# Left queries of dilated heads on two key blocks, slot sums with the dispatch weights stationary, and 512-wide early w2 products

## The chip, the cores and the metric

The kernel runs on one core of a Trainium2 chip. The metric is the device time of one execution in microseconds (us). The kernel before takes 181.05 us, the median of three runs (180.69, 181.05 and 181.62). Inputs and the result lie in HBM as 32-bit floats; the kernel works on 16-bit floats, and the transfers convert.

## The reference

A sliding-window attention is followed by a soft mixture of experts. Eight batches, eight heads, 576 positions, head dimension 64. Heads 0 to 3 ("plain") see the last 32 positions; heads 4 to 7 ("dilated") see every fourth of the last 128.

```python
scores = scale * np.matmul(q, k.transpose(0, 1, 3, 2))
mask_plain = (rel >= 0) & (rel < window)                               # window 32
mask_dil = (rel >= 0) & (rel < window * dilation) & (rel % dilation == 0)   # dilation 4
attn = softmax of the masked scores
x = (attn @ v), rows (batch, position), 512 columns: head by head

logits = x @ phi                       # 4608 x 32: 8 experts with 4 slots each
d = softmax of logits over the rows    # dispatch
slot_input = d.T @ x                   # 32 x 512
slot_out[e] = np.maximum(slot_input[e] @ w1[e], 0.0) @ w2[e]   # w1: 512 x 1024, w2: 1024 x 512
c = softmax of logits over the slots   # combine
return c @ slot_out                    # 4608 x 512
```

In bytes: q, k and v are 9.4 MB each, w1 and w2 together 33.6 MB, the result 9.4 MB.

## The kernel before

**Loads.** Every load of q, k, v and the weights is issued by POOL, and converts to 16 bits on the way; a load or store waits on POOL's queue for the data it needs, for the buffer it fills, and for the transfer issued eight before it, since there are eight completion semaphores. The order is fixed by the program: raw q, k and v of batches 0 and 1, then those of batch b+2 as the transposes of batch b free the raw buffers, one w1 matrix after each batch from the fourth, and after batch 7 the rest of the weights. w2 of experts 5 to 7 come in column halves: first the left halves of all three, then the right halves.

**Attention.** DVE transposes the raw tiles in 32x32 blocks (`turn`, L222), so that the head dimension lies on the partitions. PE turns v back into rows of keys (`v_rows`, L237, through the rotating PSUM buffers `ring`), and ACT copies them beside a column of ones into `vX`. Scores come in nine pieces per batch: P0 to P4 are 128 keys of the plain heads and the up to 160 queries that see them; D0 to D3 are every fourth key of the first 512, from residue r, with the 144 queries of that residue; L is the "left" piece, the last 64 keys of the dilated heads with the last 64 queries, reordered by residue. Three groups of pieces (`GROUPS`) share one PSUM tile each (L263), one exponential on ACT (L272) and one product with a 0/1 mask on DVE (L283).

`emit_av` (L292 to L321) multiplies the probabilities, as stationary operand, with the rows of `vX`. The ones give the sum of the row, which `emit_recip` (L325) inverts and `norm_mult` (L328 to L346) applies, on ACT for some pieces and on DVE for others; the results are the rows of x in `xp` (plain) and `xd` (dilated). The left queries of the dilated heads see keys of their residue in the D pieces (columns 128 to 143) and in L. That gives 32 small products per batch: for each head and residue one with 64 keys of L and one with 128 keys of D, 16 columns wide.

**Experts' front.** PE transposes x (`xT_plain`, `xT_dil`), ACT copies it, PE forms the logits, and ACT their exponentials `ET` (slots on partitions). For the slot sums `back_erow` (L409) turns `ET` back into rows, with the left queries a second time by residue; `back_er` multiplies with a mask, and DVE transposes the dilated order (`back_erd`, L434). `back_u` (L437) makes 25 products per batch: a 128x128 block of x stationary, 32 columns of weights moving, and five with a block of ones for the sum of the weights. The sums, with x's columns on the partitions, are added up in `UT`.

**Order.** `ORDER` (L48) is a list written by hand: each entry is a step and the iteration by which it lags; all engines' instructions are issued in that order.

**The end.** After the last batch the slot inputs are normalised into `siTm` (L593 to L606), then come the products with w1 (L616), ReLU, a transpose, and the products with w2 (`emit_so`, L641): experts 0 to 3 and 4 as soon as those are loaded, in two column halves, then 5, 6 and 7 for the left half. `gather_so` and `spread_so` sum four partial results. `emit_batch` (L689) forms the result rows of one batch, scales them on ACT and DVE in turn (L681, L685), and POOL issues the store (L692). The right halves of experts 5 to 7 are worked in between these batches; left halves of six batches are stored first, then their right halves, then batches 6 and 7 whole, and last the left queries' rows (L721).

Of the kernel before, what the change touches and what calls it, by code (L numbers as in the profile page):

```python
# [17 lines left out]
S = 576  # L18
# [14 lines left out]
NV = 10  # L33
# [3 lines left out]
DW = 144  # L37
LEFT = SUB - 128
# [6 lines left out]
    (("P", 3), ("P", 4), ("L", 0), ("D", 0)),  # L45
# [12 lines left out]
WIDTH = {"P": PW, "L": DIL * LEFT, "D": DW}  # L58


def piece_w(kind, i):
    return S - 512 if (kind, i) == ("P", 4) else WIDTH[kind]

# [15 lines left out]
def make_consts():  # L79

    a = np.arange(128)[:, None]
    rel = np.arange(PW)[None, :] - a
    band = (rel >= 0) & (rel < WINDOW)
    one = np.ones((1, N_SLOTS), bool)
    r, i = np.divmod(np.arange(DIL * LEFT)[None, :], LEFT)
    parts = [band, (a < 64) & (a % DIL == r) & (a // DIL <= i)]
    parts.append(((a % 32) < LEFT) & one)
    parts.append((a < 64) & one)
# [7 lines left out]
def kernel(  # L96
# [18 lines left out]
    band, lmask = cst[:, 0:PW], cst[:, PW : PW + DIL * LEFT]  # L115
    o_em = PW + DIL * LEFT
    o = o_em + 2 * N_SLOTS
# [4 lines left out]
    emask = consts.tile([128, 6, N_SLOTS], FP16, name="emask")  # L122
    phi_raw = consts.tile([128, 4, N_SLOTS], FP16, name="phi_raw")
    phi4 = consts.tile([128, 4, 4, N_SLOTS], FP16, name="phi4")
    ones = consts.tile([128, 128], FP16, name="ones")
    ET = consts.tile([128, 192 * B], FP16, name="ET")
    UT = consts.tile([128, 5, N_SLOTS], FP32, name="UT")
    rcol = consts.tile([128, N_SLOTS], FP32, name="rcol")
# [27 lines left out]
    x_pool = tc.alloc_tile_pool(name="xp", bufs=2)  # L156
# [12 lines left out]
    def build_masks():  # L169
# [8 lines left out]
        for kind, i in GROUPS[1]:  # L178
            w = piece_w(kind, i)
            copies(o, lmask if kind == "L" else band, w, 1)  # L180
            o += w
        nc.scalar.copy(
            out=emask[:, 4:6, :], in_=cst[:, o_em : o_em + 2 * N_SLOTS].rearrange("p (t s) -> p t s", t=2)
        )
# [39 lines left out]
    V_PARTS = ((0, 1, 2), (3, 4), (5, 6, 7), (8, 9))  # L224

    def v_rows(b, part):
        tiles = V_PARTS[part]
        rg = ring.tile([128, len(tiles), 4, 2, 32], FP16, name=f"rv_{b}_{part}", tag="ring")
        for n_t, t in enumerate(tiles):
            for c in range(2):  # L230
# [4 lines left out]
                else:  # L235
                    rows = vT[:, 1, 512:SK, c]
# [10 lines left out]
    def emit_scores(b, g):  # L247
        kb, qb = kT[b % 2], qT[b % 2]
        sps = psum_s.tile([128, 4, 512], FP32, name=f"s_{b}_{g}", tag="s")
        for kind, i in GROUPS[g]:  # L250
            c0, w = PIECE[(kind, i)][1], piece_w(kind, i)
            for tt in range(2):
                for h in range(4):
# [5 lines left out]
                    elif kind == "D":  # L259
                        kk, qq = kt[:, i:512:DIL], qt[:, i:S:DIL]  # L260
                    else:
                        kk, qq = kt[:, 512:SK], qt[:, 512:S].rearrange("p (i r) -> p r i", r=DIL)
# [11 lines left out]
    def emit_mask(b, g):  # L274
# [4 lines left out]
        else:  # L279
            m = masks[:, 0 : GW[0]].rearrange("p (n w) -> p n w", n=3)[:, :, 0:DW]  # L280
            m = m[:, None, :, :].broadcast_to([128, 4, 3, DW])
# [8 lines left out]
    xp_t, xd_t = {}, {}  # L290

    def emit_av(b, kind, i):  # L292
        o = psum_o.tile([128, 4, D + 1], FP32, name=f"o_{b}_{kind}{i}", tag="o")
        jobs, vb = [], vX[b % 2]
        for h in range(4):
            if kind == "L":
                for r in range(DIL):
                    p = probs(b, "L", 0, h, LEFT * r, 32)[0:64]
                    jobs.append((slice(32 * r, 32 * r + 32), p, vb[0:64, 9, h, 0 : D + 1], h))
            else:  # L300
                lhs = probs(b, kind, i, h, 0, 128)
                jobs.append((slice(0, 128), lhs, vb[:, i + (NP if kind == "D" else 0), h, 0 : D + 1], h))
        for h in range(4):
# [3 lines left out]
            elif kind == "L":  # L307
                for r in range(DIL):
                    lhs = probs(b, "D", r, h, 128, LEFT)
                    rows = slice(32 * r, 32 * r + LEFT)  # L310
                    jobs.append((rows, lhs, vb[:, NP + r, h, 0 : D + 1], h))
        for n, (rows, lhs, rhs, h) in enumerate(jobs):
# [4 lines left out]
                start=(n == 0 or (kind == "L" and n < DIL)),  # L317
# [5 lines left out]
    def emit_recip(b, kind, i, o):  # L323
        rc = s_pool.tile([128, 4], FP32, name=f"rc_{b}_{kind}{i}", tag=f"rc{kind}{i}")
        nc.vector.reciprocal(out=rc, in_=o[:, :, D])  # L325
        return rc

    def norm_mult(b, kind, i, o, rc, engine):  # L328
        pool, name = (xp_t, "xp") if kind == "P" else (xd_t, "xd")
        if b not in pool:  # L330
            pool[b] = x_pool.tile([128, 5, 4 * D], FP16, name=f"{name}_{b}", tag=name)
        dst = pool[b][:, 4 if kind == "L" else i, :]
        dst = dst.rearrange("p (c h d) -> p h c d", c=2, h=4)
        src = o[:, :, 0:D].rearrange("p h (c d) -> p h c d", c=2)
        if engine is nc.scalar:
# [8 lines left out]
            in1=rc[:, :, None, None].broadcast_to([128, 4, 2, D // 2]),  # L344
# [6 lines left out]
    def x_half(b, kind, t, c):  # L351
        return (xp_t if kind == "P" else xd_t)[b][:, t, 128 * c : 128 * c + 128]

    def xT_plain(b, c):
        rg = ring.tile([128, 640], FP16, name=f"rp_{b}_{c}", tag="ring")
        for t in range(NP):
            nc.tensor.transpose(rg[:, 128 * t : 128 * t + 128], x_half(b, "P", t, c), ident)  # L357
        return rg

    def xT_dil(b, c):  # L360
        rg = ring.tile([128, DIL, 160], FP16, name=f"rd_{b}_{c}", tag="ring")
        for r in range(DIL):
            nc.tensor.transpose(rg[:, r, 0:128], x_half(b, "D", r, c), ident)
        nc.tensor.transpose(rg[:, :, 128:160], x_half(b, "D", DIL, c), ident)
        return rg

    def xT_copy(b, kind, c, rg):
# [3 lines left out]
        if kind == "P":  # L371
            copy(out=xT_t[b][:, c, :], in_=rg[:, 0:S])  # L372
# [3 lines left out]
            in_=rg[:, :, 0:SUB].rearrange("p r i -> p i r"),  # L376
# [33 lines left out]
    def back_erow(b):  # L410
        m, l = et_cols(b)
        ep = ring.tile([128, 6, N_SLOTS], FP16, name=f"ep_{b}", tag="ring")
        left = ET[0:32, l : l + 128]
# [3 lines left out]
        nc.tensor.transpose(ep[:, 5, :], left, ident[0:32, 0:32])  # L417
        for r in range(DIL):
            nc.tensor.transpose(
                ep[32 * r : 32 * r + 32, 4, :],  # L420
                left.rearrange("p (i r) -> p r i", r=DIL)[:, r, :],
                ident[0:32, 0:32],
            )
        return ep

    def back_er(b, ep):
        er = s_pool.tile([128, 6, N_SLOTS], FP16, name=f"er_{b}", tag="er")
# [332 lines left out]
```

## Time and profile before

| what | before |
|---|---|
| median of three runs | 181.05 us |
| the profiled execution: its time, its span | 180.9 us, 178.9 us |
| busy: PE, DVE, ACT, POOL | 128.0, 125.7, 122.2, 56.2 us |
| PE: matmuls and as many weight loads | 2,316 |
| left rows of dilated heads (`o_L`, L313): matmuls | 256, 5.2 us |
| slot sums (`u`, L451): matmuls | 200 |
| early and late w2 products (`so`, L646): matmuls | 128 |
| HBM read, written | 62.07 MB, 9.44 MB |

The span runs from the first to the last instruction on the core. Busy times are unions: two instructions of one engine that overlap count once. A matmul's duration holds its way through the array, so matmuls of 200 ns can follow each other every 40 ns. The page has a row for the DMA engines: the core has 16 of them, and each transfer is spread over all; bytes are counted as they are in the 16-bit form for loads.

### The profile page before, as it was taken

How to read it: one execution, taken by the hardware profiler on the slowest of the kernel's cores; microseconds unless marked ns; L12 is line 12 of the kernel's file. 1: busy time of each engine (PE TensorE's matmuls, PEld its weight loads, DVE VectorE, ACT ScalarE, POOL GpSimd, SP SyncE). 2: the span in 40 equal slices, each digit the busy share in tenths (PEclk: the TensorE clock that was granted, in tenths of full speed). 3: DMA queues.
4: the chain of work that ended last, by engine and by line, in shares of the span. 5: the costliest groups of instructions: out<-in, count | busy, mean ns of one | idle time of the engine just before them, and what ended most of it. 6: DMA issues, size and time to landing. Idle time of an engine off the chain costs nothing.

```text
span 178.9 us, 5405 instructions
## 1 busy us (share of the span) xinstructions
PE 128.0 (72%) x2316; PEld 84.7 (47%) x2316; DVE 125.7 (70%) x274; ACT 122.2 (68%) x267; POOL 56.2 (31%) x94
## 2 busy tenths in 40 slices
PE   0026838989999999989989999988695346688100
PEld 0014525676667767657767757856434112221000
DVE  6483999999999999999999995472402016789200
ACT  6007757999999999999999999966002016698100
POOL 7544244224224223243420041111112414376400
PEclk9999999999999879999999999687669955555555
DMA  5999999999999999999999999999999999999994
GB/s 91 203 213 208 214 212 210 214 212 216 214 212 213 215 212 215 214 212 216 210 214 215 212 218 220 215 216 220 211 212 191 197 196 219 390 319 397 406 413 135
DMA packets 21448, 40.88 MB, mean 229 GB/s; under 512 B 1713, under 2 KB 14129, under 8 KB 20785
## 3 DMA queue, kind: packets, MB, share of 16 engines
q0 software_dynamic: 21280, 40.41, 114.2%
q8 instruction: 18, 0.29, 0.6%
q1 hardware_dynamic: 144, 0.14, 0.3%
q14 instruction: 6, 0.04, 0.1%
HBM read 62.07 MB, written 9.44 MB: 400 GB/s over the span
## 4 chain that ended last, share of the span: by engine, by line
DMA 52%; DVE 16%; PE 11%; ACT 9%; issue 3%; POOL 2%; POOLq 0%; DVEq 0%
DMA w<-in_moe_w_dram 36%; DMA rawV<-in_v_dram 10%; DMA rawK<-in_k_dram 6%; DVE vT L222 5%; DVE qk L222 4%; DVE p L283 3%; PE f L672 3%; ACT p L272 3%; ACT om L681 2%; PE s L263 2%; PE o_P L313 2%; PE rv L237 2%; ACT xp L337 1%; PE rp L357 1%; ACT vX L243 1%
## 5 line engine op out<-in xcount | busy, mean ns | idle before, releaser
L272 ACT ACTIVATE p<-s 128x1728 f16<-128x1728 f32 (+1 forms) x24 | 42.0, 1749 | 10.7 <-PE s L263 10.6
L263 PE MATMUL s<-qk 32*128 32x144 f16 (+2 forms) x640 | 29.2, 325 | 16.1 <-DVE qk L222 12.3
L313 PEld LDWEIGHTS <-p 128*128 128x128 f16 (+3 forms) x672 | 23.9, 101 | 14.0 <-issue 3.6
L263 PEld LDWEIGHTS <-qk 32*128 32x128 f16 x640 | 17.0, 118 | 20.4 <-DVE qk L222 12.3
L337 ACT ACTIVATE xp<-o_P,rc_P 128x64 f16<-128x64 f32 x96 | 23.8, 384 | 2.4 <-DVE rc_P L325 2.3
L283 DVE TENSOR_TENSOR p<-p,masks 128x1728 f16<-128x1728 f16 (+1 forms) x24 | 25.4, 1082 | 0.0
L243 ACT COPY vX<-rv 128x512 f16<-128x512 f16 (+1 forms) x32 | 23.5, 786 | 1.7 <-PE rv L237 1.6
L313 PE MATMUL o_P<-vX,p 128*128 128x65 f16 (+1 forms) x288 | 20.7, 210 | 1.3 <-DVE xp L341 0.3
L222 DVE STREAM_TRANSPOSE qk<-rawQ 128x576 uint32<-128x576 uint32 x16 | 18.9, 1243 | 2.7 <-DMA rawQ<-in_q_dram 2.7
L222 DVE STREAM_TRANSPOSE qk<-rawK 128x576 uint32<-128x576 uint32 x16 | 19.7, 1241 | 0.5 <-DMA rawK<-in_k_dram 0.5
L222 DVE STREAM_TRANSPOSE vT<-rawV 128x576 uint32<-128x576 uint32 x16 | 19.6, 1238 | 0.4 <-DMA rawV<-in_v_dram 0.4
L237 PE MATMUL rv<-cst,vT 128*128 128x128 f16 x160 | 17.3, 248 | 3.0 <-DVE vT L222 1.7
L211 POOL DMA_DIRECT2D w<-in_moe_w_dram x12 | 8.9, 745 | 29.1 <-DMA w<-in_moe_w_dram 24.8
L685 DVE TENSOR_SCALAR om<-f,rrow 128x256 f16<-128x256 f32 (+1 forms) x28 | 13.5, 518 | 3.9 <-PE f L672 3.1
L237 PEld LDWEIGHTS <-vT 128*128 128x128 f16 x160 | 12.0, 127 | 8.6 <-issue 4.3
L191 POOL DMA_DIRECT2D rawQ<-in_q_dram x16 | 8.9, 557 | 21.5 <-DVE rc_P L325 16.3
L681 ACT ACTIVATE om<-f,rrow 128x256 f16<-128x256 f32 (+1 forms) x28 | 12.8, 503 | 3.3 <-PE f L672 2.6
L672 PE MATMUL f<-so_sb,ET 32*128 32x256 f16 (+1 forms) x60 | 12.1, 420 | 3.7 <-ACT om L681 2.4
L692 POOL DMA_DIRECT2D out_dram<-om x14 | 10.4, 747 | 12.1 <-DVE om L685 9.4
L191 POOL DMA_DIRECT2D rawK<-in_k_dram x16 | 8.7, 548 | 17.1 <-DVE rc_P L325 14.6
L191 POOL DMA_DIRECT2D rawV<-in_v_dram x16 | 8.7, 547 | 10.8 <-DVE rc_P L325 8.0
L372 ACT COPY xT<-rp 128x576 f16<-128x576 f16 x16 | 10.5, 776 | 1.2 <-PE rp L357 1.2
(84 smaller groups left out, 197.4 us busy)
## 6 DMA issues: line engine op xcount, KB each, us to landing
w<-in_moe_w_dram POOLq DMA_DIRECT2D x13, 1024.0 KB, 21.7
out_dram<-om POOLq DMA_DIRECT2D x12, 512.0 KB, 6.2
rawQ<-in_q_dram POOLq DMA_DIRECT2D x16, 288.0 KB, 10.7
rawK<-in_k_dram POOLq DMA_DIRECT2D x16, 288.0 KB, 10.4
rawV<-in_v_dram POOLq DMA_DIRECT2D x16, 288.0 KB, 10.2
w<-in_moe_w_dram POOLq DMA_DIRECT2D x12, 256.0 KB, 16.4
out_dram<-om POOLq DMA_DIRECT2D x2, 1024.0 KB, 8.6
out_dram<-om_l POOLq DMA_DIRECT2D x2, 512.0 KB, 9.1
```

Source lines behind the costliest of these rows:

```text
L191: nc.gpsimd.dma_start(out=t[g::2, :], in_=src[4 * g : 4 * g + 4].rearrange("h (p j) d -> (h p) (j d)", j=PJ),)
L222: nc.vector.transpose(out=out_, in_=in_)
L237: nc.tensor.transpose(rg[:, n_t, :, c, :], rows, ident)
L243: copy(out=vX[b % 2][:, t0 : t0 + n, :, 0:D], in_=rg.rearrange("p n h c d -> p n h (c d)"))
L263: nc.tensor.matmul(sps[:, h, c0 : c0 + w], kk, qq, start=(tt == 0), stop=(tt == 1))
L272: return nc.scalar.activation(out=pt, in_=sps[:, :, 0:n], func=AF.Exp, scale=SCALE)
L283: return nc.vector.tensor_tensor(out=pt, in0=pt, in1=m, op=ALU.mult)
L313: nc.tensor.matmul(o[rows, h, :], lhs, rhs, start=(n == 0 or (kind == "L" and n < DIL)), stop=(n == len(jobs) - 1), skip_group_check=True,)
L337: nc.scalar.activation(out=dst[:, h], in_=src[:, h], func=AF.Copy, scale=rc[:, h : h + 1])
L672: nc.tensor.matmul(fp[:, 0 : c1 - c0], ET[32 * j : 32 * j + 32, m : m + 128], so_sb[32 * j : 32 * j + 32, c0:c1], start=True, stop=True,)
L681: nc.scalar.activation(out=dst, in_=fp[:, 0 : c1 - c0], func=AF.Copy, scale=rrow[:, blk : blk + 1])
L685: nc.vector.tensor_scalar(out=dst, in0=fp[:, 0 : c1 - c0], scalar1=rrow[:, blk : blk + 1], scalar2=None, op0=ALU.mult)
```

## The change

Four things are done, and the constants follow them.

- The left queries of the dilated heads are scored in natural order against two blocks of 128 keys, from 448 and from 384, as two pieces of group 1 (`LKEY`); the D pieces have 128 queries each. The second block counts only its first 64 keys. `v_rows` makes two row tiles for them where there was one, and `emit_av` needs 8 products per batch, into 64 rows.
- Rows that hold only 64 positions are computed as 64, and the transposes of x follow. x lies in fixed tiles with a column of ones behind its 256 columns.
- In `back_u` the dispatch weights are the stationary operand, and x with its ones is the moving one, 257 columns wide: 10 products per batch into 64 rows, plain and dilated below each other. The sums lie with slots on partitions, so at the end they are normalised by a column, transposed by PE, and copied into `siTm` by DVE (plain) and ACT (dilated).
- The w2 products of experts 0 to 4 are 512 columns wide, into one PSUM tile; experts 5 to 7 stay in halves.

```diff
-    (("P", 3), ("P", 4), ("L", 0), ("D", 0)),
+    (("P", 3), ("P", 4), ("L", 0), ("L", 1), ("D", 0)),
...
-WIDTH = {"P": PW, "L": DIL * LEFT, "D": DW}
+WIDTH = {"P": PW, "L": LEFT, "D": 128}
+LKEY = (448, 384)
...
-    V_PARTS = ((0, 1, 2), (3, 4), (5, 6, 7), (8, 9))
+    V_PARTS = ((0, 1, 2), (3, 4), (5, 6, 7), (8, 9, 10))
...
-                    rows = vT[:, 1, 512:SK, c]
+                    k0 = LKEY[t - NP - DIL]
+                    rows = vT[:, 1, k0 : k0 + 128, c]
...
-                    kk, qq = kt[:, 512:SK], qt[:, 512:S].rearrange("p (i r) -> p r i", r=DIL)
+                    kk, qq = kt[:, LKEY[i] : LKEY[i] + 128], qt[:, 512:S]
...
             if kind == "L":
-                for r in range(DIL):
-                    p = probs(b, "L", 0, h, LEFT * r, 32)[0:64]
-                    jobs.append((slice(32 * r, 32 * r + 32), p, vb[0:64, 9, h, 0 : D + 1], h))
+                for n in range(2):
+                    k = 128 if n == 0 else 64
+                    lhs = probs(b, "L", n, h, 0, LEFT)[0:k]
+                    jobs.append((slice(0, LEFT), lhs, vb[0:k, NP + DIL + n, h, 0 : D + 1], h))
...
-            elif kind == "L":
-                for r in range(DIL):
-                    lhs = probs(b, "D", r, h, 128, LEFT)
-                    rows = slice(32 * r, 32 * r + LEFT)
-                    jobs.append((rows, lhs, vb[:, NP + r, h, 0 : D + 1], h))
...
-        nc.tensor.transpose(ep[:, 5, :], left, ident[0:32, 0:32])
-        for r in range(DIL):
-            nc.tensor.transpose(
-                ep[32 * r : 32 * r + 32, 4, :],
-                left.rearrange("p (i r) -> p r i", r=DIL)[:, r, :],
-                ident[0:32, 0:32],
-            )
+        nc.tensor.transpose(ep[:, 4, :], ET[0:32, l : l + 128], ident[0:32, 0:32])
...
-        nc.vector.tensor_tensor(out=er, in0=ep, in1=emask, op=ALU.mult)
+        nc.vector.tensor_copy(out=er, in_=ep)
...
-        up = ring.tile([128, 5, N_SLOTS], FP32, name=f"u_{b}", tag="ring")
+        up = ring.tile([64, 4 * D + 1], FP32, name=f"u_{b}", tag="ring")
...
+            for k, x in enumerate((xp_t[b % 2], xd_t[b % 2])):
+                e = erd[:, t, :] if k == 1 and t < 4 else er[0:n, t, :]
+                nc.tensor.matmul(
+                    up[32 * k : 32 * k + 32, :],
+                    e,
+                    x[0:n, t, 0 : 4 * D + 1],
+                    start=(t == 0),
+                    stop=(t == NP - 1),
+                )
...
+    nc.vector.reciprocal(out=rcol, in_=U[:, 4 * D : 4 * D + 1])
+    nc.vector.tensor_scalar(out=si, in0=U[:, 0 : 4 * D], scalar1=rcol, scalar2=None, op0=ALU.mult)
+    for k, copy in enumerate((nc.vector.tensor_copy, nc.scalar.copy)):
+        siT = ring.tile([128, 2, N_SLOTS], FP16, name=f"siT{k}", tag="ring")
+        rows = slice(32 * k, 32 * k + 32)
+        for c in range(2):
+            nc.tensor.transpose(siT[:, c, :], si[rows, 128 * c : 128 * c + 128], ident[rows, rows])
...
+        copy(out=diag, in_=siT.rearrange("p c (e s) -> p c e s", e=E_EXP))
...
-    so = [psum_so.tile([128, DH], FP32, name=f"so{s}", tag=f"so{s}") for s in range(2)]
+    so = psum_so.tile([128, DMODEL], FP32, name="so", tag="so")
...
-    for s in range(2):
-        emit_so(s, (0, 1, 2, 3))
-    for s in range(2):
-        emit_so(s, (4,))
+    emit_so(None, (0, 1, 2, 3))
+    emit_so(None, (4,))
     for e in (5, 6, 7):
         emit_so(0, (e,))
```

More of the change, by code (lines that the diff above doesn't have):

```diff
@@ L32 @@
 PJ = S // PB
-NV = 10
+NV = 11
 SUB = S // DIL
@@ L83, in make_consts @@
     band = (rel >= 0) & (rel < WINDOW)
[L84 to L88, printed above, removed]
+    parts = [band]
+    for first in LKEY:
+        rel = 512 + np.arange(LEFT)[None, :] - first - a
+        seen = LKEY[0] if first < LKEY[0] else S
+        parts.append((rel >= 0) & (rel < WINDOW * DIL) & (rel % DIL == 0) & (first + a < seen))
     parts.append(a == np.arange(128)[None, :])
@@ L114 @@
     cst = consts.tile([128, consts_np.shape[1]], FP16, name="cst")
[L115 to L117 removed]
+    o = PW + 2 * LEFT
+    band, lmask = cst[:, 0:PW], [cst[:, PW + LEFT * i : PW + LEFT * i + LEFT] for i in range(2)]
     ident = cst[:, o : o + 128]
@@ L316, in emit_av @@
                 rhs,
-                start=(n == 0 or (kind == "L" and n < DIL)),
+                start=(n == 0),
                 stop=(n == len(jobs) - 1),
@@ L371, in xT_copy @@
         if kind == "P":
-            copy(out=xT_t[b][:, c, :], in_=rg[:, 0:S])
+            copy(out=xT_t[b][:, c, :], in_=rg)
             return
```

126 lines of the change are left out of this document (55 added, 71 removed).

## Prediction

> **What bounds the kernel now.** I read the summary page first: the slices of the span, the DMA queues and the issue table.
>
> ```profile
> span 178.9 us, 5405 instructions
> PEclk9999999999999879999999999687669955555555
> DMA  5999999999999999999999999999999999999994
> GB/s 91 203 213 208 214 212 210 214 212 216 214 212 213 215 212 215 214 212 216 210 214 215 212 218 220 215 216 220 211 212 191 197 196 219 390 319 397 406 413 135
> q0 software_dynamic: 21280, 40.41, 114.2%
> q8 instruction: 18, 0.29, 0.6%
> ...
> w<-in_moe_w_dram POOLq DMA_DIRECT2D x13, 1024.0 KB, 21.7
> ...
> rawQ<-in_q_dram POOLq DMA_DIRECT2D x16, 288.0 KB, 10.7
> rawK<-in_k_dram POOLq DMA_DIRECT2D x16, 288.0 KB, 10.4
> rawV<-in_v_dram POOLq DMA_DIRECT2D x16, 288.0 KB, 10.2
> ```
>
> The DMA row is full in all slices but the first and the last. A 288 KB load lands 10 us after its issue, yet loads land 1.4 us apart: some 8 us of work always stand queued ahead of it. So the transfers are the bound, and an engine matters only if it lets that queue run dry. The chain of waits says the same of the last third: weights back to back until 153.58, then a short run through the engines.
>
> ```profile
> 88.68 28.72 DMA w<-in_moe_w_dram
> 117.40 0.28 issue
> 117.68 25.39 DMA w<-in_moe_w_dram
> 143.08 0.28 issue
> 143.36 10.22 DMA w<-in_moe_w_dram
> 153.58 0.04 issue
> 153.62 0.43 PE so L646 x4
> ```
>
> Next, the completion marks in the trace: each transfer leaves 16, one for each DMA engine. This is the lag of the engines behind the first to finish, in order (us), for three loads, and then the marks of three outputs by their absolute time:
>
> ```
> load issued  22.23: 0.00 0.03 0.05 0.12 0.13 0.17 0.22 0.29 0.38 0.39 0.45 0.47 0.48 0.53 0.60 1.29
> load issued 117.68: 0.00 0.13 0.26 0.28 0.31 0.51 1.09 1.17 2.13 2.26 2.41 2.62 2.68 2.69 2.81 3.66
> load issued 143.36: 0.00 0.11 0.27 0.29 0.31 0.52 1.11 1.19 2.15 2.27 2.42 2.63 2.69 2.70 2.82 3.47
> output 5, issued 154.14: 1st 157.63, 14th 159.58, 15th 160.26, last 160.63
> output 6, issued 157.61: 1st 160.62, 14th 160.98, 15th 161.66, last 161.88
> last output, issued 167.93: 1st 176.13, 14th 176.46, 15th 177.10, last 177.39
> ```
>
> The engines carry equal bytes but drift apart. What differs are the 18 instruction packets of queue 8, 16,384 bytes and about 0.94 us each on one engine. They start at 22.1, 35.0, 42.5 and so on to 128.6, 140.7 and 154.0, each after about 256 further PE instructions (4,649 in the program). After the first, one engine is 0.7 us late; after seven, seven engines are; after sixteen, eight are late by 2.1 to 2.8. The 17th, at 140.7, makes one of these 3.66 late, and the 18th, at 154.0, holds up a second. So refills go round eight engines, and the two that were hit three times land last to the end. They never wait for an issue, so their load sets the time.
>
> **The change, part by part.** By the instruction listing of the two programs, the transfers, their order and what each waits for are the same. The constants stay 548 columns wide. So the byte floor does not move. What moves:
>
> PE instructions. Per batch, pairs of weight load and matmul: left rows 32 to 8 (-24), left scores +8, V transposes +2, transposes of the dispatch weights 6 to 2 (-4), slot sums 25 to 10 (-15), in all -33. Over eight batches -264; early w2 products 80 to 40 (-40); four new transposes (+4): -300 pairs, -600 instructions, 4,649 to 4,049. At 256 per refill that is 15.8, so 15 or 16 refills instead of 18. The 17th and 18th, the two that give an engine a third hit, do not happen. Without the 17th the worst lag at the end of the loads is 2.82 instead of 3.47: -0.65 us. Without both, the end is set by what is now the third slowest engine: at output 5 it is 160.63 - 159.58 = 1.05 ahead, at the last output 177.39 - 176.46 = 0.93 (from output 6 on it is partly held by the issues, so this is a lower bound). I take -1.0 us. A 16th refill, if there is one, is the second hit of the eighth engine, which it had before, and costs nothing.
>
> The Trainium skill, on the page "Runtime: NRT & Kernel Launch", section Instruction fetch mechanics, says that instructions are refilled in 16 KiB blocks of 256 and that crossing a block boundary is "mostly hidden"; by that the refills are worth nothing and the time would stay at 181.05. The block size agrees with the packets here; the hiding does not agree with the marks, since these transfers share engines that have no idle time.
>
> Work per batch on the engines, all of it beside the transfers. PE: the left rows took 0.67 us by the chain, about 0.2 after; slot sums 0.8 us before, and 10 products of 257 columns at 0.1 us (four 256-wide products took 0.40 at half clock) 0.5 to 1.0 after; two V transposes +0.2, four fewer small ones -0.2; eight more 64-wide scores +0.25 (3.9 us for 128), 32 narrower ones about -0.25. PE gains 0.3 to 0.8. ACT: the widths of the three exponentials sum to the same (1,344); one V copy grows from 512 to 768, 892 - 680 ns = +0.21 us. DVE: the sum over 257 columns takes at most the 0.40 of a 256-wide product instead of 0.30, `er` about 0.04 less, masks sum to the same. So a batch is 0.2 us longer at most if ACT sets its pace, 1.7 us over eight. Cover: the 8 us of queue; loads per batch take 6 x 1.4 + 4.9 = 13.3 us against some 12.9 between issues now. The added memsets (about 0.09 us each) replace two of 0.22 and 0.17 before the first load lands.
>
> The front of the expert part, once. The reciprocal and the product on 128 rows (0.35 + 0.29 us) become a reciprocal (0.17), a product of 256 columns (0.40), two transposes (0.25 each), a copy (0.27), and for the second half a wait of PE for the buffer that `rs` holds until DVE has read it (0.37), two more transposes, an ACT copy (0.27). That is about 2.0 us plus hops: +1.4 to +2.0. Behind PE's wait stand all w1 products. The 512-wide products move the same columns as before; at full clock nothing, at the 0.50 granted around them at most +1.5 us. With 0 to 1.7 us from the batches, the early products end later by d = 1.4 to 5.2 us. PE's own timeline shows the cover:
>
> ```profile
> 137.03 2.79 PE L646 MATMUL so<-w,hTm 128*32 128x256 f16 x88 [0.52 <-DVE hTm L628]
> 140.94 0.29 PE L646 MATMUL so<-w,hTm 128*32 128x256 f16 x4 [1.11 <-DMA w<-in_moe_w_dram]
> 143.12 0.38 PE L646 MATMUL so<-w,hTm 128*32 128x256 f16 x4 [1.88 <-DMA w<-in_moe_w_dram]
> 144.26 0.40 PE L646 MATMUL so<-w,hTm 128*32 128x256 f16 x4 [0.76 <-DMA w<-in_moe_w_dram]
> 145.64 0.41 PE L646 MATMUL so<-w,hTm 128*32 128x256 f16 x4 [0.98 <-DMA w<-in_moe_w_dram]
> ```
>
> That is 4.7 us of waiting for weights; 4.05 when they land 0.65 earlier. Then the first output, issued at 149.31, may be later too. Output 6 shows that an idle engine lands 3.0 us after an issue, 1.3 of it the transfer; the slowest engine is free at about 152.9, so an issue by 151.2 costs nothing: 1.9 more. Cover is lost at d = 6.0. I cost the front at nothing.
>
> After the last weight lands, the steps to output 6 are unchanged, so it should be issued 0.65 us earlier, at about 156.96; the slowest engine then ends output 5 at 159.6 and needs it by 157.9.
>
> Sum: 180.9 us of the profiled execution (span 178.9, 2.0 around it) less 1.0 is 179.9. The median of the runs, 181.05, is 0.15 above that execution: 180.05.
>
> **Rivals.**
> Refills hidden or replaced: lighter engines lose slack that I don't see, or other queues fill the place. For it: the instruction queue has 0.6% of the DMA time; against it: the jumps of 0.7 to 1.0 us in the marks. 181.05.
> One hit only: a different start of the round, or a refill late in the output phase, leaves one engine with a third hit; only 0.65 is won: 180.4. For it: the 18th refill came when PE had started 4,564 instructions, so the counting is loose by some tens; against it: 4,049 is 303 short of a 17th refill.
> Compute gets faster and the kernel follows: against it, no load waits for anything but the queue; no time of its own.
> Slower: the front of the expert part outlasts its cover. PE stands behind the new transposes and the first output comes late. It decides from d = 6.0 us, and each further us is a us on all output; at d = 8.5, 180.05 + 2.5 = 182.55. For it: PE's clock fell to 0.50 there, and ACT and DVE are busy without a gap from 36 to 108 us; against it: my worst d is 5.2, and PE is relieved in every batch.
>
> **How the numbers follow.** The three runs of before span 0.5%, and 0.5% (0.9 us) is about what a measurement of this kernel can tell from no change; the forecast stands just beyond that, at -0.55%. Chances: forecast 0.49 (its own range 179.6 to 180.3), one hit only 0.18, hidden refills 0.22, slower 0.11. So faster by over 0.5% 0.49, within 0.5% 0.40, slower 0.11. The range reaches from 179.5 (the gain at 1.05 and half of the spread of the runs) to 181.5 (hidden refills and the same spread); it leaves out most of the slower case.
>
> **What would show it.** Queue 8 with 15 or 16 packets; worst lag of the last load near 2.8; last weight near 152.9, last output near 176.4; all loads still 1.4 and 4.9 us apart. If PE no longer waits for `w` before the last early products, the slower case has come. Refills down with the last landing unmoved would make the central step wrong; so would a load that lands late after its issue into an empty queue.

## The result, and the profile after

The changed kernel takes 184.89 us, the median of six runs (181.99 to 187.23); the kernel before, run beside it, 180.9 us (180.68 to 181.62). The ratio is 1.0106, with a 95% interval of 1.006 to 1.0152. A second set gave 184.14 us (four runs, 182.91 to 186.09) against 181.2, a ratio of 1.0141 (1.0099 to 1.0184). The ratios leave out the runs that count as slow (four of the change's six here, one of its four in the second set), which is why they lie below the ratios of the medians, 1.022 and 1.016. So the change makes the kernel slower by 1.0 to 1.4% by the ratios and by 1.6 to 2.2% by the medians, where 0.55% faster was forecast. The runs spread over 5 us, where those of before spread over 1.

The profiled execution is the fastest of the six, 181.99 us. These are the lines of its summary page that answer those shown of before, with PE's busy time and its busy slices, and the shares of the chain of waits by engine:

```profile
span 180.1 us, 4810 instructions
...
PE 136.0 (75%) x2016; PEld 87.9 (49%) x2016; DVE 127.1 (71%) x277; ACT 125.2 (69%) x268; POOL 56.2 (31%) x94
...
PE   0015938999998998999899999998977687688000
...
PEclk9999999955999999987987955899955898555555
DMA  5999999999999999999999999999999999999994
GB/s 101 189 207 209 211 213 212 211 214 216 213 213 215 213 211 213 214 213 213 211 217 214 213 216 224 218 215 209 220 207 191 196 196 144 402 354 393 406 412 111
...
q0 software_dynamic: 21280, 40.41, 113.6%
q8 instruction: 16, 0.26, 0.5%
...
PE 39%; ACT 28%; DVE 13%; DMA 9%; issue 3%; POOL 1%; POOLq 0%; ACTq 0%; DVEq 0%
...
w<-in_moe_w_dram POOLq DMA_DIRECT2D x13, 1024.0 KB, 20.8
...
rawQ<-in_q_dram POOLq DMA_DIRECT2D x16, 288.0 KB, 10.1
rawK<-in_k_dram POOLq DMA_DIRECT2D x16, 288.0 KB, 8.6
rawV<-in_v_dram POOLq DMA_DIRECT2D x16, 288.0 KB, 9.0
```

Three things are to be seen. Queue 8 has 16 packets, as forecast. But PE is busy for 136.0 us with 2,016 products, where it was 128.0 with 2,316: a product has become dearer. And the clock row, which stood at 9 through most of the attention before (8 and 7 in two slices, lower at its end), now has more gaps, at the ninth and tenth slice and from the eighteenth on, while PE's own row stands at 8 or 9 there. The GB/s row has its answer in slice 34: 144, where it was 219.

The chain of waits ran through the transfers for 52% of the span before; now that is 9%, and PE has 39%. At the end of the attention and in the front of the expert part it reads:

```profile
132.82 0.34 ACT ET L408
133.21 0.29 PE ep L413
133.67 0.25 DVE er L421
133.97 1.39 PE u L437 x10
135.38 0.43 DVE U L451
...
137.15 5.61 PE hps L605 x53
...
145.43 3.03 PE so L636 x64
148.48 0.30 DVE so_part L651
...
150.00 0.47 ACT om L672
```

These are compute steps one behind the other, with no wait for a weight between them. PE's timeline shows the same place (start, duration, and in brackets the idle time before and what ended it):

```profile
137.08 5.64 PE L605 MATMUL hps<-w,siTm 128*32 128x512 f16 x64
...
145.43 3.00 PE L636 MATMUL so<-w,hTm 128*32 128x512 f16 x64 [0.52 <-DVE hTm L617]
```

The early w2 products start at 145.43 instead of 137.03, so d, the delay that the prediction put at 1.4 to 5.2 us, is 8.4. They run as one block of 64, with the left halves of experts 5 to 7 in it: no wait for `w` is left of the 4.7 us that stood here. That is the sign that the prediction named for the slower rival.

What became of the transfers is in their completion marks (us):

```
                                          before    after
last weight load, last mark               153.58   152.97
worst lag of one engine in that load        3.47     2.81
output 1, issued                          149.31   151.54
output 1, last mark                       154.97   154.95
output 5, last mark                       160.63   160.15
output 6, issued                          157.61   158.61
output 6, last mark                       161.88   161.88
output 8, last mark                       164.54   164.56
output 9, last mark                       165.92   167.12
last output, last mark                    177.39   178.64
instruction packets of queue 8           18, last at 154.0    16, last at 164.6
```

The loads end 0.6 us earlier, as the refill step said. Then output 1 is issued 2.2 us later: all engines have run dry by then, its marks lie within 0.37 us instead of 2.7, and the gain is gone. Output 6, issued 1.0 us later, meets a second hole, which before had stood on the faster engines alone: now the slowest one is free at 160.15, too. After eight outputs the two kernels are level to 0.02 us. The remaining 1.2 us come at one step, between outputs 8 and 9: there the 16th instruction packet, at 164.6, occupies one engine for 1.04 us. At output 8 the 16 marks lie within 0.28 us; from output 9 to the end one mark stays 0.9 to 1.2 us behind the other fifteen.

### The profile page after: what moved, and what is told of

The parts are those of the page before. It is cut to its first block, busy times and chain, and to the rows that moved or that the text cites. A ratio compares the mean times of both kernels' runs of the same rounds, so it can differ in the third digit from the quotient of the medians.

```text
span 180.1 us, 4810 instructions
## 1 busy us (share of the span) xinstructions
PE 136.0 (75%) x2016; PEld 87.9 (49%) x2016; DVE 127.1 (71%) x277; ACT 125.2 (69%) x268; POOL 56.2 (31%) x94
## 4 chain that ended last, share of the span: by engine, by line
PE 39%; ACT 28%; DVE 13%; DMA 9%; issue 3%; POOL 1%; POOLq 0%; ACTq 0%; DVEq 0%
ACT p L271 10%; PE s L262 7%; DMA phi_raw<-in_moe_phi_dram 5%; PE o_L L307 5%; ACT xp L331 5%; PE f L663 4%; DVE qk L220 4%; ACT xT L374 4%; PE o_P L307 4%; DMA rawK<-in_k_dram 4%; PE u L437 3%; PE hps L605 3%; ACT vX L242 3%; ACT om L672 3%; PE rv L236 3%
## 5 line engine op out<-in xcount | busy, mean ns | idle before, releaser
L271 ACT ACTIVATE p<-s 128x1920 f16<-128x1920 f32 (+1 forms) x24 | 41.4, 1726 | 12.5 <-PE s L262 12.3
L262 PE MATMUL s<-qk 32*128 32x128 f16 (+2 forms) x704 | 28.7, 314 | 17.6 <-DVE qk L220 12.7
L307 PEld LDWEIGHTS <-p 128*128 128x128 f16 (+2 forms) x480 | 27.8, 107 | 14.7 <-issue 3.1
L262 PEld LDWEIGHTS <-qk 32*128 32x128 f16 x704 | 18.7, 125 | 20.2 <-DVE qk L220 12.7
L331 ACT ACTIVATE xp<-o_P,rc_P 128x64 f16<-128x64 f32 x96 | 23.3, 368 | 4.0 <-DVE rc_P L320 3.9
L242 ACT COPY vX<-rv 128x768 f16<-128x768 f16 (+1 forms) x32 | 24.6, 810 | 1.8 <-PE rv L236 1.8
L282 DVE TENSOR_TENSOR p<-p,masks 128x1920 f16<-128x1920 f16 (+1 forms) x24 | 25.3, 1079 | 0.0
L307 PE MATMUL o_P<-vX,p 128*128 128x65 f16 (+2 forms) x288 | 21.1, 212 | 0.4 <-DVE xd L335 0.2
L236 PE MATMUL rv<-cst,vT 128*128 128x128 f16 x176 | 17.9, 245 | 3.0 <-DVE vT L220 1.8
L236 PEld LDWEIGHTS <-vT 128*128 128x128 f16 x176 | 13.3, 125 | 7.4 <-issue 3.7
L683 POOL DMA_DIRECT2D out_dram<-om x14 | 10.4, 745 | 14.0 <-DVE om L676 11.5
L672 ACT ACTIVATE om<-f,rrow 128x256 f16<-128x256 f32 (+1 forms) x28 | 12.8, 502 | 2.4 <-PE f L663 1.7
L189 POOL DMA_DIRECT2D rawV<-in_v_dram x16 | 8.7, 548 | 11.5 <-DVE rc_P L320 8.6
```

Of the source, the lines that this page charges most:

```text
L189: nc.gpsimd.dma_start(out=t[g::2, :], in_=src[4 * g : 4 * g + 4].rearrange("h (p j) d -> (h p) (j d)", j=PJ),)
L236: nc.tensor.transpose(rg[:, n_t, :, c, :], rows, ident)
L242: copy(out=vX[b % 2][:, t0 : t0 + n, :, 0:D], in_=rg.rearrange("p n h c d -> p n h (c d)"))
L262: nc.tensor.matmul(sps[:, h, c0 : c0 + w], kk, qq, start=(tt == 0), stop=(tt == 1))
L271: return nc.scalar.activation(out=pt, in_=sps[:, :, 0:n], func=AF.Exp, scale=SCALE)
L282: return nc.vector.tensor_tensor(out=pt, in0=pt, in1=m, op=ALU.mult)
```

## The experiments

The first theory after the trace was that PE loses time where stationary operands with 128 and with 64 rows alternate. `emit_av` now takes, head by head, a product with 128 rows of the first `L` block and one with 64 rows of the second. PE's timeline, in a middle batch of before and of after:

```profile
73.42 0.53 PE L313 MATMUL o_L<-vX,p 64*32 64x65 f16 x32
```

```profile
76.73 1.24 PE L307 MATMUL o_L<-vX,p 128*64 128x65 f16 x8
77.90 0.30 PE L307 MATMUL o_D<-vX,p 128*128 128x65 f16 x4
```

Thirty-two products, sorted by their rows, took 0.53 us; eight that alternate take 1.24. The rivals: the half clock alone; the new slot sums; the wide w2 products; refills that were costed wrongly; neighbouring products that add into the same PSUM rows and wait for each other; and ACT as the engine that sets the pace of a batch. The table has all runs. "Batch" is the mean distance of the exponentials of the logits (`ET`) of one batch from those of the next, from start to start, over the first five distances; "`o_L`" the time from each left product's start to the next instruction's start on PE, added up per batch (mean of three middle batches); "half clock" the time at a granted clock of 0.50 between 20 and 130 us; d is counted from 137.03. "Last output" is its last completion mark. These come from the one profiled execution of each.

| kernel | median (runs), us | ratio to before, 95% | batch | `o_L` | half clock | d | refills, last at | last output |
|---|---|---|---|---|---|---|---|---|
| before | 180.9 (6) | 1 | 12.84 | 0.46 | 14.1 | 0 | 18, 154.0 | 177.39 |
| the change | 184.89 (6) | 1.0106 (1.006 to 1.0152) | 13.81 | 1.17 | 27.3 | 8.4 | 16, 164.6 | 178.64 |
| the change, again | 184.14 (4) | 1.0141 (1.0099 to 1.0184) | 13.75 | 1.24 | 26.0 | 9.2 | 16, 165.9 | 179.56 |
| `l128` | 181.26 (10) | 1.0016 (0.9982 to 1.005) | 12.87 | 0.37 | 9.2 | 2.1 | 16, 163.5 | 177.48 |
| `lord` | 182.57 (1) | | 13.36 | 0.52 | 35.8 | 9.0 | 16, 165.5 | 179.22 |
| `all128` | 180.28 (10) | 0.9969 (0.9957 to 0.9982) | 12.91 | 0.37 | 2.3 | 1.1 | 16, 163.4 | 177.06 |
| `pad100` | 179.91 (4) | 0.994 (0.9917 to 0.9963) | 12.89 | 0.37 | 0.1 | 0.9 | 16, 142.3 | 176.28 |
| `pad228` | 180.47 (10) | 0.9973 (0.9958 to 0.9988) | 12.89 | 0.37 | 28.1 | 4.0 | 17, 145.9 | 177.44 |
| `hps2` | 179.99 (4) | 0.9939 (0.9918 to 0.996) | 13.12 | 0.44 | 11.5 | 6.6 | 16, 151.7 | 176.83 |
| `all128_so` | 179.97 (5) | 0.9942 (0.9919 to 0.9965) | 13.15 | 0.44 | 6.8 | 2.1 | 16, 155.6 | 177.29 |
| `b_so` | 181.37 (10) | 1.002 (1.0006 to 1.0034) | 12.79 | 0.46 | 14.7 | 0.2 | 18, 161.9 | 177.25 |
| `b_alt` | 209.78 (4) | 1.1542 (1.1472 to 1.1612) | 17.11 | 4.79 | 41.0 | 35.5 | 18, 183.1 | 207.02 |

**One row count in the left products (`l128`).** The second block's probabilities are zero in rows 64 to 127, by the mask; the product now runs over them too.

```diff
-                    k = 128 if n == 0 else 64
+                    k = 128
```

> The changed kernel, but the second left key block is multiplied over all 128 rows (its masked rows are zero, so nothing else changes): the 8 left products of a batch no longer alternate between 128 and 64 rows. They took 1.17 us per batch on PE from start to start, against 0.46 for the 32 before. Theory 'row switch' (PE empties itself whenever the number of stationary rows changes): 0.3 to 0.5 us, a batch 12.8 to 12.9 us instead of 13.45, the w1 products start 5 us earlier than 137.1, time 180.0 to 180.8. Theory 'same rows' (two products in a row add into the same PSUM rows and wait for each other): 1.17 and 13.45 stay, time 182 to 187 as now. Theory 'ACT' (the V copy that grew by 0.21 us and the wider second exponential set the pace): the left products may shrink, but a batch stays at 13.3 or more.

The eight products now take 0.44 us in the timeline:

```profile
74.03 0.28 PE L437 MATMUL u<-xp,er 64*32 64x257 f16 x1
74.03 0.28 PE L437 MATMUL u<-xd,er 64*32 64x257 f16 x1
74.25 0.44 PE L307 MATMUL o_L<-vX,p 128*64 128x65 f16 x8
```

The batch is back at 12.87 us, d falls from 8.4 to 2.1, and the ratio to before from 1.0106 and 1.0141 to 1.0016, with an interval that meets neither of theirs. More rows per product, and less time: it is not the work. The neighbours still add into the same PSUM rows, ACT's copies and exponentials are those of the change, and so are the slot sums, the w2 products and the number of refills, so none of these explains what went. Whether it is the alternation or the products with 64 rows themselves, the next run tells.

The median, 181.26 us, lies above the 180.0 to 180.8 that were expected, and the runs still spread from 180.29 to 183.74. The mean granted clock, on record for each run, parts them: 0.818 to 0.876 in the five of 180.29 to 180.84 us, 0.788 to 0.807 in the three of 181.68 to 182.84.

**The same eight products, sorted (`lord`).** Four with 128 rows, then four with 64.

```diff
             if kind == "L":
-                for n in range(2):
-                    k = 128 if n == 0 else 64
-                    lhs = probs(b, "L", n, h, 0, LEFT)[0:k]
-                    jobs.append((slice(0, LEFT), lhs, vb[0:k, NP + DIL + n, h, 0 : D + 1], h))
+                lhs = probs(b, "L", 0, h, 0, LEFT)
+                jobs.append((slice(0, LEFT), lhs, vb[:, NP + DIL, h, 0 : D + 1], h))
...
+            elif kind == "L":
+                lhs = probs(b, "L", 1, h, 0, LEFT)[0:64]
+                jobs.append((slice(0, LEFT), lhs, vb[0:64, NP + DIL + 1, h, 0 : D + 1], h))
```

> The changed kernel with the left products in another order: first the four of 128 rows, then the four of 64. 'Row switch': two changes of rows per batch instead of eight, so 0.5 to 0.7 us per batch and a batch of 12.9 to 13.1. 'Same rows': no two neighbours share rows, so 0.3 to 0.5 us. 'ACT': a batch stays at 13.3 or more. A theory that products of 64 rows are slow in themselves: 0.8 or more.

```profile
74.25 0.55 PE L308 MATMUL o_L<-vX,p 128*64 128x65 f16 x8
```

Products with 64 rows are not slow in themselves: sorted, the eight take 0.49 us in this batch to the start of what follows. With two changes of row count that is 0.12 above the 0.37 of `l128`, which has none; alternating, with eight, it is 0.80 above.

From product to product the traces are clearer than these sums. At full clock the next product starts 0.03 to 0.05 us after the one before it where the shape stays, and 0.12 to 0.15 us after it where the rows change, in the change and in `lord` alike. The last step of `l128`, to `o_D`, takes 0.13 us too: there the rows stay at 128 and the columns go from 64 to 128. So a change of shape costs about 0.1 us, and the 0.37 of `l128` holds one as well.

But the one run, 182.57 us, is no gain over the profiled run of the change. The first three batches take 12.87 to 12.94 us; the next three, under a granted clock of 0.50 from 87 to 94 and from 101 to 142 us, 13.94 to 14.29. So there is a second cause beside the changes' own time, the clock. One run with a 41-us stretch can't say how often that comes.

**No product with 64 rows left (`all128`).** As `l128`, and the slot sums and the transposes of x take 128 rows too; the last tile of x has zeros in rows 64 to 127. The scores keep their 32 rows, as in every kernel here.

```diff
     def x_half(b, kind, t, c):
-        n = LEFT if t == 4 else 128
+        n = 128
...
         for t in range(NP):
-            n = LEFT if t == 4 else 128
+            n = 128
             for k, x in enumerate((xp_t[b % 2], xd_t[b % 2])):
...
+            nc.vector.memset(x[64:128, 4, :], 0.0)
...
```

> As the run with 128 rows for the left products, and the products and transposes that work on the 64 rows of the last tile (slot sums, transposes of x) work on 128 rows too, with zeros in rows 64 to 127; no change of rows is left in attention. 'Row switch': another 0.2 us per batch off the slot sums and 0.3 off the transposes of the dilated x, where each stands between products of 128 rows; a batch of 12.5 to 12.8, time 179.7 to 180.5. The other theories: the same time as the run with the left products alone.

The median falls to 180.28 us, faster than before by 0.18 to 0.43%. The batch did not get shorter: 12.91 us, where 12.5 to 12.8 was expected, so that part of the theory failed. What went with it is half clock, 2.3 us in the trace where the change had 27.3 and `l128` 9.2. The runs agree: their mean granted clock is 0.86 to 0.89 in all ten, against 0.79 to 0.88 in the ten of `l128` and 0.77 to 0.84 in the ten of the change. The page's clock row is clean up to the expert part:

```profile
PEclk9999999999999999999999999999858675555555
```

The last load lands at 153.06, but the 16th refill still comes at 163.4.

**Row changes alone, in the kernel before (`b_alt`).** If the changes are the cause, they must hurt the old kernel too. It has 16 left products with 64 rows and then 16 with 128; here the same 32 alternate.

```diff
...
             if kind == "L":
                 for r in range(DIL):
                     p = probs(b, "L", 0, h, LEFT * r, 32)[0:64]
                     jobs.append((slice(32 * r, 32 * r + 32), p, vb[0:64, 9, h, 0 : D + 1], h))
+                    lhs = probs(b, "D", r, h, 128, LEFT)
+                    rows = slice(32 * r, 32 * r + LEFT)
+                    jobs.append((rows, lhs, vb[:, NP + r, h, 0 : D + 1], h))
...
-            elif kind == "L":
...
-                start=(n == 0 or (kind == "L" and n < DIL)),
+                start=(n == 0 or (kind == "L" and n in (2, 4, 6))),
```

> The kernel before with the same 32 left products per batch in another order: each of 64 rows is followed by one of 128 rows, instead of sixteen and then sixteen. 'Row switch': each change costs 0.10 us ((1.17 - 0.37) / 8 from the changed kernel and the run with 128 rows), 31 changes instead of one, so the left products take 0.46 + 3.0 = 3.5 us, a batch 14.5 us or more, the w1 products start 10 us or more later than 128.5, beyond the cover, and the time is 184 to 190. 'Same rows' (neighbours that add into the same PSUM rows): only half of the neighbours share rows; 1.5 us and half the loss, 181 to 184. If the count of products or of instructions mattered: nothing changes, 181.0.

It takes 209.78 us: 28.6 us more for another order of the same products. The page, and then the left products of one batch in PE's timeline:

```profile
span 208.5 us, 5405 instructions
...
PEclk9999999589579769859958967975755576955555
DMA  6999999999959969988999999999999200299995
```

```profile
68.98 4.84 PE L311 MATMUL o_L<-vX,p 64*32 64x65 f16 x32
```

The left products take 4.79 us per batch instead of 0.46: 4.33 for 30 more changes, 0.14 us each, the larger part at half clock. From product to product it is 0.13 us at full clock and 0.15 to 0.16 at half. The rival of shared PSUM rows had 1.5 us for all 32. The batch grows by 4.28 us, to 17.11, the transfers can't hide that, and they run dry (2 and 0 in the DMA row). In each of the first six batches stands one stretch of 6.8 us at half clock, at 36.0, 53.1, 70.2, 87.2, 104.3 and 121.4, one each 17.1 us. The expectation's direction held; its size, 184 to 190 us, was far too small.

**The wide w2 products alone, in the kernel before (`b_so`).**

```diff
...
-    for s in range(2):
-        emit_so(s, (0, 1, 2, 3))
-    for s in range(2):
-        emit_so(s, (4,))
+    emit_so(None, (0, 1, 2, 3))
+    emit_so(None, (4,))
```

> The kernel before with one part of the change alone: the w2 products of experts 0 to 4 are 512 wide in one PSUM tile (4,569 PE instructions). No theory of the slowdown touches it: attention as before, a batch 12.83 us. 'A refill costs': 17 refills, or an 18th at the very end; between no change and 0.4 us faster, 180.6 to 181.0. If the wide products themselves were slow, the early w2 products would take over 3.5 us instead of 2.8, still ahead of the weights: no change either.

Ratio 1.002: hardly slower. The products start at 137.24, so the wide form isn't what made the front late. With 80 instructions fewer there are still 18 refills, and the last has moved from 154.0 to 161.9, into the outputs. The median, 181.37, is above the 180.6 to 181.0 that were expected.

**Where the refills fall (`pad100`, `pad228`).** `all128` with 100 or 228 pairs of a weight load and a tiny product on zeros at the start, where PE waits for data anyway. They move every later refill forward; 228 make a 17th.

```diff
     load_raw("V", 1)
+    zz = consts.tile([128, 32], FP16, name="zz")
+    nc.vector.memset(zz, 0.0)
+    for _ in range(100):
+        dm = ring.tile([32, 32], FP32, name="dm", tag="ring") if _ == 0 else dm
+        nc.tensor.matmul(dm, zz, zz, start=True, stop=True)
```

> The kernel without changes of rows (180.28 us, 4,049 PE instructions) plus 100 weight loads and 100 tiny products on zeros at the start, while PE waits for the first load; they do not touch the result. In that kernel the 16th refill comes at 163.4 us, in the output phase, when all DMA engines have just been brought level, and the last output ends 1.1 us behind the next engine. With 200 instructions more it should come some 200 instructions from the end, near 145 us, on an engine that had one hit and has slack. Theory 'a refill costs its DMA engine time, and only where that engine is the last': 1.0 us faster with more instructions, 179.0 to 179.5. Theory 'refills are hidden': 180.3, no change.

> The same with 228 pairs, 4,505 PE instructions: the 17th refill comes about 200 instructions from the end and is the third hit of one engine before the last load. 'A refill costs': 0.6 to 0.7 us more than with 100 pairs, 179.7 to 180.1, worst lag of the last load 3.3 to 3.7. 'Hidden': as with 100 pairs.

With 200 useless instructions more the kernel is faster than `all128` by a little: 179.91 us against 180.28 in the median, 0.994 of before (0.9917 to 0.9963) against 0.9969 (0.9957 to 0.9982), intervals that just touch, and 176.28 against 177.06 in the last output's mark. Its 16th refill comes at 142.3, among the loads, and no refill meets the outputs. This is the lowest median of all kernels here; `hps2` and `all128_so` lie within its interval. The expectation had 1.0 us to win, from a last mark 1.1 us behind the others. That lag is the change's (178.64 against 177.54); in `all128` it is 0.54, and the trace gives back 0.78. Its page, and then the early w2 products in PE's timeline:

```profile
span 177.8 us, 5019 instructions
...
PEclk9999999999999999999999999999969965555555
...
q8 instruction: 16, 0.26, 0.5%
```

```profile
137.92 2.56 PE L642 MATMUL so<-w,hTm 128*32 128x512 f16 x48 [0.52 <-DVE hTm L623]
140.75 0.29 PE L642 MATMUL so<-w,hTm 128*32 128x256 f16 x4 [0.27 <-DMA w<-in_moe_w_dram]
142.13 0.29 PE L642 MATMUL so<-w,hTm 128*32 128x256 f16 x4 [1.09 <-DMA w<-in_moe_w_dram]
143.42 0.32 PE L642 MATMUL so<-w,hTm 128*32 128x256 f16 x4 [1.00 <-DMA w<-in_moe_w_dram]
```

PE waits for weights again. With 128 pairs more, the 17th refill comes at 145.9 and gives one engine its third hit: that engine is 3.86 us late at the last load (2.68 in `pad100`), the load lands 1.11 us later, the last output 1.16 later, and the median is 0.56 higher, above the 179.7 to 180.1 that were expected (the intervals of the ratios overlap slightly). This is the step by which the prediction costed the 17th and 18th refill of before. `pad228` also had 28 us at half clock, but most of that, 11 to 38 us, lies before the batches of the table.

**How much the cover holds (`hps2`).** `all128` with all products with w1 made twice, the second over the first.

```diff
-    for fc in range(2):
+    for fc in (0, 1, 0, 1):
```

> The kernel without changes of rows, in which all products with w1 are made twice, to the same result: the front of the expert part is 5.6 us longer. In that kernel the w1 products start 0.7 us later than before the change, so the early w2 products come d = 6.3 us late. By the prediction's cover of 6.0 us: 0 to 0.5 us lost, 179.5 to 180.8 (the 16th refill also moves ahead of the outputs). If the cover is smaller, as 4.0: 2 us or more lost, 181.3 or more. If the front has nothing to do with the time: 179.3.

The early w2 products start at 143.63, d = 6.6, and nothing is lost: 179.99 us. The second pass cost less than I had expected, 8.78 us for both against 5.29 in `pad100` and 5.64 in the change for one; the first begins at half clock, which ends at 135.6:

```profile
132.14 8.78 PE L606 MATMUL hps<-w,siTm 128*32 128x512 f16 x128
143.63 3.00 PE L637 MATMUL so<-w,hTm 128*32 128x512 f16 x64 [0.52 <-DVE hTm L618]
```

Here too the 64 products stand in one block without a wait for weights, and output 1 is issued at 149.74. So the loss of those waits alone is not yet a loss of time. With sixty-four products more the median is 0.29 below `all128` (the intervals overlap), and they bring the 16th refill to 151.7, before the loads end.

**The change, run again (`after_again`).** No edit.

> The changed kernel once more, on the same chip as the run with the alternating order, for its spread and its clock: 182 to 187 us. If the granted clock adds to the row switches, the profile shows batches of 13.4 us where the clock is full and of 14.2 to 14.8 where it is 0.50, and the w1 products start between 135 and 140 us.

The medians differ by 0.75 us, the profiled runs by 0.92. The last output goes with d, run by run: 8.4, 9.0 (`lord`) and 9.2 give 178.64, 179.22 and 179.56. So a microsecond of d is about a microsecond of time here. Followed back to the 177.06 of `all128`, whose 16th refill comes as late, this begins at d = 8.4 - 1.6 = 6.8, and `hps2` lost nothing at 6.6.

**Early w2 products in halves in the good kernel (`all128_so`).** The halves lie in one PSUM tile and disturb each other's sums there, so this kernel's w2 products are not the reference's; their number and sizes are those of before.

```diff
-    emit_so(None, (0, 1, 2, 3))
-    emit_so(None, (4,))
+    for s in range(2):
+        emit_so(s, (0, 1, 2, 3))
+    for s in range(2):
+        emit_so(s, (4,))
```

> The kernel without changes of rows with one more part undone: the early w2 products in halves (4,129 PE instructions). The 16th refill comes 80 instructions earlier, near 158 us, still among the outputs. 'A refill costs': 180.0 to 180.4, as with wide products (180.28). If the wide products had a price of their own: 179.8 or less.

179.97 us against 180.28: the wide form brings nothing of its own. The 80 instructions more bring the 16th refill from 163.4 to 155.6, the last output stands at 177.29 and not below `all128`, and the median is 0.31 lower. Here trace and median point in different directions, by about as much as such runs spread.

## Why the prediction was wrong

**Work per batch: the step that failed.** It took the left rows from 0.67 us to "about 0.2 after", had PE gain "0.3 to 0.8", and let a batch grow by 0.2 us at most. I counted products and never asked what an alternation of shapes costs, although the listing showed 128 and 64 rows in turn. The left products went from 0.46 to 1.17 us, and a batch at full clock from 12.74 to 13.43. Of these 0.69 us, `l128`, with every other edit in place, gives back 0.56 (12.87). They are eight changes of row count per batch, about 0.1 us each; `b_alt` shows the same in the old kernel, 0.14 us each, mostly at half clock. The 0.13 us that stay in `l128` would fit the 0.2 at most that the prediction gave to ACT, but were not followed up. The 0.67 us of the prediction are a reading of the first and the last batch; the six between took 0.46. The Trainium skill, on the page "TensorEngine Tiling (Array Packing)", section Tiling Modes, says "Mode switching requires drain"; it gives no price. The runs agree with it; the prediction had not weighed it.

**The clock: a term that was missing.** Half clock adds to this. A batch that meets it takes up to 14.7 us. The time at 0.50 between 20 and 130 us was 27 us with the change, 9 without its left row changes, 2 without any of 64 rows, and `b_alt` has a stretch in every batch. That half clock goes with the row changes of `l128`, `all128` and `b_alt` is shown, by the traces and by the mean clocks of the runs; what starts a stretch is not. `pad228` had 28 us without a product of 64 rows, before had 14, and `lord`, with few changes, 36. The Trainium skill, on the page "TensorE: Matmul & The Clock Gate", section HAM oscillation — how this bites in real kernels, ties the half clock to waits of PE between bursts of products, idle gaps of over about 3.4 us. This case's traces do not agree: in the 6.8 us before each stretch that starts between 30 and 110 us, the longest gap in PE's records is 0.33 us in the change, 0.05 in `b_alt` and 0.40 in any trace. Whether a change of shape counts as idle time no run here shows.

**The front of the expert part.** I put it at +1.4 to +2.0 us; from the last addition to the slot sums to the first product with w1 it is 1.09 us before and 1.70 after, +0.6. This term was too large, and the batches' term, 0 to 1.7 us, far too small: the last slot sum is 7.95 us late, 1.7 of it before the first `ET` and 5.8 between the first and the last. So d is 8.4 and not 5.2 at most.

**The cover.** "Cover is lost at d = 6.0" was close: 6.6 costs nothing in `hps2`, 8.4 opens two holes. The slower rival came by its own mechanism: its formula, 180.05 + (d - 6.0), gives 182.45 for d = 8.4, and the profiled run took 181.99. That the two lie so close is in part luck, since the formula has no price for the 16th refill. I gave it 0.11, since "PE is relieved in every batch"; PE is what had got slower.

**The refills.** The step itself was right: 16 packets, worst lag 2.81 (2.82 forecast), last weight at 152.97 (152.93 forecast). "A 16th refill ... costs nothing" was wrong. It was costed as a second hit of an engine in the lagging round of the loads; but it falls at 163 to 166 us, when the late first output has just brought all engines level, and then whichever engine it takes is the last one. In the profiled run that step is the whole net loss against before, 1.2 us, the late front having eaten the 0.6 won at the loads. In `all128`, whose first output is not late and whose marks still lie 0.91 us apart at output 8, a refill at the same place costs about 0.6 us: from output 8 to 9 it takes 1.91 us, where `pad100` takes 1.34.

**The sum.** With the row changes gone and the 16th refill out of the outputs, `pad100` takes 179.91 us, where I forecast 180.05 and the last output near 176.4 (176.28). So a gain of the size that I read from the profile is there; the change as it was made does not get it.

**What stays open.** No trace exists of the runs at 186 to 187 us. On record of them is a low mean granted clock, 0.773 to 0.795, where the three at 184.10 to 184.37 have 0.837; but 0.816 and 0.815 belong to the fastest two, so the clock alone does not order the runs, and their d is not known. POOL's pause of over 2 us before output 6, in both kernels, was not looked into.

## What to carry to other kernels

Count the changes of stationary shape, not only the products: eight products that alternate between 128 and 64 rows cost more here than 32 that are sorted, and zero rows that keep one shape are the cheaper way. A kernel that hides behind its transfers has a cover of so many microseconds, and a small cost in each batch must be multiplied by the batches before it is called hidden. Where all DMA engines are full, ask not only how many instruction refills there are but when each comes; one late in a phase where the engines run level is paid in full.

## What the runs showed of the hardware that I had not expected

- At full clock, a change between 128 and 64 rows of the stationary operand puts the next product 0.12 to 0.15 us after the one before it, where products of one shape follow each other in 0.03 to 0.05. Sorting the same 32 products by rows is worth 28.6 us in 209.78.
- A granted clock of 0.50 comes in stretches of 3.4 us and multiples (3.4, 6.8, 10.2, 27.3, 41.0), also where PE's records show no gap over 0.40 us in the 6.8 us before.
- A refill of PE's instructions takes its DMA engine 0.89 to 1.09 us (one in `b_alt` 1.41). In this kernel 200 added instructions, which moved the refills forward, go with 0.4 us less in the median, and 256 more, which added one, with 0.56 more.
